# Block 1's gate weights in seven half products, and another order of the work beside them, in a fused linear attention and gated MoE kernel

## Chip, cores and metric

The kernel runs on one core of a Trainium2 chip. The metric is the time of one execution on the device, in microseconds (us), as the median of several runs. Before the change the median of three runs is 318.88 us (318.71 to 319.47). One execution is also taken by the hardware profiler; its timeline, waits and DMA records are what this document reads. The engines are TensorE (PE; PEld is its weight load), VectorE (DVE), ScalarE (ACT), GpSimd (POOL) and SyncE (SP, which issues DMAs here).

## The reference

For each of 8 batches, q, k and v have 8 heads, 576 rows and 64 columns. A linear attention comes first, then a gated feed-forward layer over all 4608 tokens:

```python
kv = np.einsum('bhsd,bhse->bhde', k, v)   # k'v of each head
out = np.einsum('bhsd,bhde->bhse', q, kv)
rms = np.sqrt(np.mean(out * out, axis=-1, keepdims=True) + 1e-06)
x = out / rms * g_norm              # 4608 x 512 after the heads are put side by side
g = x @ w_gate                      # 512 x 1536
gelu = 0.5 * g * (1.0 + erf(g * inv_sqrt2))
val = x @ w_val
ffn_out = gelu * val @ w_out        # 1536 x 512
res_gate = 1.0 / (1.0 + np.exp(-(x @ w_res)))   # w_res is 512 x 512
return x + res_gate * ffn_out
```

## The kernel before

**Blocks.** The tokens are worked off in nine blocks of 512: block b holds the first 512 rows of batch b, block 8 the last 64 rows of all batches. While block m goes through the feed-forward layer, the attention of batch m + 2 runs beside it: `kv_mm` (k'v, 40 matmuls of 64 columns, the last 8 of them for the last rows, tiles `kl` and `vl`), `a_o` (q times k'v, PSUM tiles `op`), `a_ss` (squares on ScalarE, sums over them on VectorE), `a_norm` (the inverse root, tile `ny`), `a_t` (op times ny, tile `t`), `d_xT` (a transpose by DMA, queued on SP) and `a_g` (the scaling by g_norm, in place in `xT`).

**Seven half products.** Where a product is split once into quadrants (Strassen's scheme in Winograd's form), seven products of half the size do what eight would, at the price of sums. `gv_group` does this for w_gate and w_val, with sums of tokens (`token_sums`, tile `ts`) and of weights (`wsg`, `wsv`). `out_by_products` does it for w_out, with sums of the hidden values (`hid_s`, functions `s_begin`, `s_sum`, `s_rest`, `s_last`) and of w_out (`wo_ts`, function `wo_sums`). `res_halves` does it for w_res, with sums of w_res (`wrs`, `wr_sums`), in the blocks from 2 on. Blocks 0 and 1 have the plain w_res product: `m_res`, 16 matmuls of 512 columns.

**Order.** The order of every engine's work is written out by hand. A block is a list of slots on TensorE; `plans[blk][slot]`, filled by `at`, names what is issued after a slot. `at_word` puts work behind a word of a group's order ("2v", "h12"), and `aside_out` ahead of one of the four output quadrants of `out_by_products` ("F", "00", "22", "01", "11", "end"). Each engine works its queue in order.

**Block 1.** Its slots are: two tiles of 128 hidden columns as plain products (0 and 1), a group of four in half products (2), six more plain ones (6 to 11, PSUM tiles `gps`, `vps`), then the output. The output begins with `res(0)` (two `m_res`), k'v of batch 3, `res(1)`, `a_o` of batch 3, and `first_two`: the product wA (hidden quadrant by w_out quadrant), its copy into the bank of wE (ScalarE), the product wD and its copy `wd`. `others` then adds to wA, wE and wF and forms the four output quadrants: on VectorE the sum into wF's bank (line 512, `wF<-wA,wd`), the sum for the last quadrant straight into the output buffer (`osb<-wA,wd`, its `c22`), and the gate products `pf` (line 733: `osb<-th,wE`, `osb<-th,wF`, `osb<-th,wA`); the fourth gate product is GpSimd's. The output buffer `res_all` (`osb`) exists once; block 0's four stores read it (`m_store`: an addition on GpSimd, then a DMA on SP), and `late` spreads them over block 1's slots.

**PSUM banks.** There are eight. `banks_behind` hands block 1's output tiles four of them, and the next block's first group takes over the same four: Ag the bank of wD, Av that of wE, Eg that of wF, Ev that of wA. Its Fg and Fv take the banks of the first two `op` tiles. In a group, product 1 goes into Ag, a copy on ScalarE brings it into Eg ("Eg"), and product 6 then adds to Ag.

```python
ORDERS = {
    None: "1g 1v Eg 5g 6g Ev 5v dg 6v dv Fg 2g Fv 2v 7g g11 7v cg 3g cv 3v h11 g12 4g g21 h12 4v g22 h21 h22",
```

Of the kernel before, what the change touches and what calls it, by code (L numbers as in the profile page):

```python
# [18 lines left out]
def kernel(  # L19
# [57 lines left out]
    def banks_behind():  # L77

        g0, v0, g1, v1 = pmoe.turn
        pmoe.turn = [g1, v0, g0, v1]  # L80
        return {0: g0, 1: g1, 2: v0, 3: g0, "A": v1, "D": g1, "E": v0, "F": g0}

    ctx.enter_context(tc.manual_schedule())
    nc.scalar.preload_act_table_set("sqrt_and_others")
# [125 lines left out]
    def kv_mm(b, ps):  # L210
        k16 = b16_t[b, "k"]
        v16 = b16_t[b, "v"]
        kl, vl = last_kv[b % 2]
        for pr in range(NP):
            for j in range(NJ + 1):
                for e in range(2):
                    h = 2 * pr + e
                    nc.tensor.matmul(  # L218
                        ps[halves(e), pr, :],
                        lhsT=k16[:, h, j * D : (j + 1) * D] if j < NJ else kl[:, h, :],  # L220
                        rhs=v16[:, h, j * D : (j + 1) * D] if j < NJ else vl[:, h, :],
                        start=(j == 0),
                        stop=(j == NJ),
                    )

    def a_kv(b, copy=nc.vector.tensor_copy):
# [260 lines left out]
        nc.vector.tensor_tensor(out=pf, in0=th, in1=fps, op=ALU.mult)  # L487
        return pf

    def m_store(blk, j, pf):  # L490
        osb = pf
        nc.gpsimd.tensor_tensor(out=osb, in0=pf, in1=t_t[blk][:, j, :], op=ALU.add)
        dst = out[blk * S : blk * S + M0, :].rearrange("(p j) c -> p j c", j=NJ)[:, j, :]
        nc.sync.dma_start(out=dst, in_=osb)

# [15 lines left out]
    def sub(eng, out_, in0, in1, op=ALU.subtract):  # L511
        eng.tensor_tensor(out=out_, in0=in0, in1=in1, op=op)

    def wo_sums(i):

        pairs = [(b_of(1, 2), b_of(1, 1)), (b_of(2, 2), wo_t[:, 0]), (b_of(2, 2), b_of(1, 2)), (b_of(2, 1), wo_t[:, 1])]
        sub(nc.vector, wo_t[:, i], *pairs[i])

    def s_begin(blk):

        s_ = hid_sums
        sub(nc.vector, s_[2], a_of(blk, 1, 1), a_of(blk, 2, 1))

    def s_rest(blk):

        s_ = hid_sums
        sub(nc.vector, s_[0], a_of(blk, 2, 1), a_of(blk, 2, 2), ALU.add)
        sub(nc.vector, s_[1], s_[0], a_of(blk, 1, 1))

    def s_sum(blk, i):  # L530

# [10 lines left out]
    def s_last(blk):  # L542
        sub(nc.vector, hid_sums[3], a_of(blk, 1, 2), hid_sums[1])
# [95 lines left out]
    def out_by_products(blk, banks, amid):  # L639
# [4 lines left out]
            for f in amid.get(ahead_of, ()):  # L644
                f()

        def res(jj):
            for j in (2 * jj, 2 * jj + 1):
                m_res(blk, j, banks[j])

        def tiles_of_w():
            for n in ("D", "E", "F", "A"):
                w[n] = pmoe.tile([P, 2, CH], FP32, name="w" + n, bank=banks[n])
# [60 lines left out]
            for jj in ((0, 0), (0, 1), (1, 1), (1, 0)):  # L714
                sigmoid(jj)

        def first_two():
            tiles_of_w()
            s_last(blk)
            prod(w["A"], a_of(blk, 1, 1), b_of(1, 1), True)  # L720
            nc.scalar.copy(out=w["E"], in_=w["A"])
            aside("D")
            prod(w["D"], s_[0], wo_t[:, 0], True)
            nc.scalar.copy(out=w["d"], in_=w["D"])
            aside("d")
            for j in range(NJ):
                m_sigmoid(j)

        def part(jj):
            return slice(None), slice(2 * jj[0], 2 * jj[0] + 2), slice(jj[1] * CH, (jj[1] + 1) * CH)  # L730
# [13 lines left out]
        def others():  # L744


            prod(w["A"], s_[1], wo_t[:, 1], False)
            aside("F")
            sub(nc.vector, w["F"], w["A"], w["d"], ALU.add)
            if res_and_attn(blk):  # L750
                s_last(blk)
            aside("00")
            prod(w["E"], a_of(blk, 1, 2), b_of(2, 1), False)
            if not whole(blk + 1):
                pf((0, 0), w["E"])
            aside("22")
            prod(w["A"], s_[2], wo_t[:, 2], False)
            c22 = res_all[part((1, 1))]
            sub(nc.vector, c22, w["A"], w["d"], ALU.add)
            if whole(blk + 1):  # L760
                pf((0, 0), w["E"])
            aside("01")
            prod(w["F"], s_[3], b_of(2, 2), False)
            pf((0, 1), w["F"])
            aside("11")
            prod(w["A"], a_of(blk, 2, 2), wo_t[:, 3], False)
            if whole(blk + 1):
                pf((1, 1), c22, nc.gpsimd)
                pf((1, 0), w["A"])
                aside("end")  # L770
            else:
                pf((1, 1), c22)
                pf((1, 0), w["A"])
            if blk + 1 == WHOLE or blk + 1 == LAST[0]:
                nc.gpsimd.tensor_copy(out=hold, in_=x_sums[blk + 1][0:1, 3, 1, 1, 0:1])
            if blk == LAST[0]:
                nc.gpsimd.tensor_copy(out=hold, in_=s_[3][0:1, 0, 0:1])
            for j in range(NJ):
                row_times_g(blk, j, nc.gpsimd)
            if blk == LAST[0]:  # L780
                for p in range(B // 2):
                    row_times_g(B, p, nc.gpsimd)
            rows_behind()
# [8 lines left out]
            return [with_res_and_attn, lambda: None, lambda: None, others]  # L792
        if res_in_halves(blk):
            return [with_res, lambda: None, lambda: None, others]
        return [lambda: res(0), lambda: res(1), first_two, others]

    def out_last(blk, banks):

# [239 lines left out]
    def out_by_f(blk):  # L1038

        ths, fpss, pfs, banks = [], [], [], {}  # L1040

        def res(j):
            if j == 0:
                banks.update(banks_behind())
            ths.append(m_res(blk, j, banks[j]))

        slots = [lambda j=j: res(j) for j in range(NJ)]

        def step(f):
            if f == 0:  # L1050
                fpss.extend(pmoe.tile([P, C], FP32, name="fps", bank=banks[n]) for n in "ADEF")
                pmoe.turn = [banks[n] for n in "ADEF"]
            for j in range(NJ):
                m_ffn(blk, j, f, fpss[j])
                for g in amid_step.get((f, j), ()):
                    g()
            if NFH <= f < NFH + NJ:
                m_sigmoid(f - NFH)
            if f == NF - 1:
                pfs.extend(m_gate(j, ths[j], fpss[j]) for j in range(NJ))  # L1060

        slots += [lambda f=f: step(f) for f in range(NF)]
        return slots, [lambda j=j: m_store(blk, j, pfs[j]) for j in range(NJ)]


    tiles_16(0)
# [338 lines left out]
    def plan_attn_2():  # L1405
        b, m = 2, 1
        act = nc.scalar.copy
        at(m - 1, 2 * NF + 3, lambda: by_token(b, act, slice(0, 2)))
        ts = token_sums(m, nc.vector)
        at(m, 0, lambda: by_token(b, act, slice(2, 4)), lambda: attn_begin(b), lambda: d_qT(b), *ts[0:2])  # L1410
        at(m, 1, *ts[2:4])
        at_word(m, 0, "dg", lambda: wo_sums(1))
        at_word(m, 0, "2v", lambda: a_kv(b, act), lambda: load_behind(b))
        at_word(m, 0, "Fv", lambda: wo_sums(2))
        at(m, NF, *late_sums[6:8])
        at(m, 2 + GF, lambda: a_o(b), *[lambda j=j: a_ss(b, j) for j in range(NJ)])
        at(m, 3 + GF, lambda: a_norm(b, 0, NJ))
        for j in range(NJ):
            at(m, 4 + GF + j // 2, lambda j=j: a_t(b, j))
        at(m, 6 + GF, lambda: d_xT(b, 0, NJ))  # L1420
        at(m, NF - 1, lambda: wo_sums(3))
        for i in range(2):
            aside_out(m, "d", lambda i=i: a_g(b, 2 * i, 2 * i + 2, nc.scalar))
        amid_out.setdefault(m, {}).setdefault("00", [])[0:0] = [wr_[3]]

    WHOLE = 2
    GROUPS = {blk: (1, 2) for blk in range(2, WHOLE)} | {blk: (0, 1, 2) for blk in range(WHOLE, B - 1)} | {B - 1: (1, 0, 2), B: (0, 1, 2)}
# [9 lines left out]
    def plan_attn_ahead(b):  # L1437
# [20 lines left out]
                at(m, 2 * GF, lambda: load_behind(b))  # L1458
            last = len(GROUPS[m]) - 1
        else:  # L1460
            at(m, 8, lambda: by_token(b, act, slice(0, 2)))
            at(m, 9, lambda: by_token(b, act, slice(2, 4)), *begin)
            at(m, NF, lambda: a_kv(b, act), lambda: load_behind(b, load_q))
            aside_out(m, "end", lambda: load_kv(b + 1))
        if rem:
            at_word(m + 2, 0, "cv", lambda: a_g(b, NJ, NJ + 1))
# [3 lines left out]
            if own:  # L1470
                at_word(m, last, "3g", lambda: rem_mm(b))
            at_word(m, last, "g12", lambda: rem_out(b))
        else:
            at(m, NF + 1, lambda: a_o(b), *[lambda j=j: a_ss(b, j) for j in range(NJ)])
        aside_out(m, "F", lambda: a_norm(b, 0, NJ + rem, pool))
        first = [lambda: new_block(b), lambda: a_t(b, 0), lambda: a_t(b, 1)]
        if whole(m + 1):
# [32 lines left out]
    for blk in GROUPS:  # L1510
        t = token_sums(blk, nc.vector)
        if blk == 2:
            aside_out(blk - 1, "00", *t[0:2])
            aside_out(blk - 1, "end", *t[2:4])
            continue
        for key, f in zip(("00", "00", "22", "end") if whole(blk) else ("00", "22", "01", "11"), t):
            aside_out(blk - 1, key, f)
# [43 lines left out]
    for blk in range(B + 1):  # L1561
        plan = plans[blk]
        if blk == 0:
# [11 lines left out]
                gv_group(0, 2, ends, amid_gv.get((0, 0), {}), True)  # L1575

            slots += [last_group, None, None, None]
            outs, stores = out_by_f(0)
            slots += outs
            plan_attn_2()  # L1580
            for b in range(3, B):
# [1 line left out]
        else:  # L1583
# [43 lines left out]
                plan.setdefault(NF - 2, []).insert(0, lambda: s_begin(blk))  # L1627

            def products(blk=blk, outs=outs):
                if not res_in_halves(blk) and not res_and_attn(blk):  # L1630
                    s_rest(blk)
                if blk not in GROUPS:
                    out_at[blk] = banks_behind()
                if blk < B:
                    outs.extend(out_by_products(blk, out_at[blk], amid_out.get(blk, {})))
                else:
# [21 lines left out]
                    load_wo(f0, f1)  # L1658
        assert not plan
        if blk == 0:  # L1660
            late = [stores[0:2], [], [], [], stores[2:3], stores[3:4]]


# [28 lines left out]
```

## Time and profile before

| what | value |
|---|---|
| median of 3 runs | 318.88 us |
| profiled execution, its own time | 318.52 us |
| its span, first to last instruction | 316.5 us |
| granted TensorE clock, mean | 0.995 |
| block 1's part: first plain product to block 2's first product | 53.26 to 89.10 us |
| w_res of block 1 on TensorE | 74.84 to 79.2 us, with k'v of batch 3 in between |
| stores of block 0, issued on SP | two at 58.6 and 59.5, two at 67.7 and 68.8 us |
| transposes on SP | qT of batch 3 at 72.2, xT of batch 2 at 75.5 us |

The span counts from the first to the last instruction. What lies around it makes up the 2.0 us to the execution's own time. In a timeline, the columns are the start in us, the duration (of a row's first start to its last end where instructions are merged), engine, line, operation, output and inputs with their shapes, the number of instructions, and in brackets the idle time ahead with what ended it. Matmuls overlap: their pace is read from the starts, not from the durations.

### The profile page before, as it was taken

The numbers are of one execution on the slowest core, as the hardware profiler recorded it, in microseconds if no ns is written. First come the engines' busy times: TensorE is split into PE (matmuls) and PEld (weight loads), VectorE is DVE, ScalarE is ACT, GpSimd is POOL, SyncE is SP. The second block draws the span as 40 slices with busy tenths as digits, with TensorE's granted clock in tenths as the row PEclk, the third lists the DMA queues.
The fourth block names the chain that finished last, engine by engine and source line by source line (L and its number), as shares of the span: only waits on it lengthen the run. The fifth ranks groups of instructions, "written<-read, shape, count | busy, mean of one in ns | idle before, by whom it ended". The sixth has DMA issues, their size and how long they took to land.

```text
span 316.5 us, 7841 instructions
## 1 busy us (share of the span) xinstructions
PE 308.2 (97%) x3071; PEld 249.1 (79%) x3071; DVE 275.7 (87%) x489; ACT 217.0 (69%) x395; POOL 187.4 (59%) x239
## 2 busy tenths in 40 slices
PE   7899999999999999999999999999999999999993
PEld 3555756844888888888888888888888888888882
DVE  5897998989898899989998999899998777897774
ACT  4764688685958794879487948795667367736760
POOL 2883352360799579856985798408850474396332
PEclk9999999999999999999999999999999999999997
DMA  7999999899969598389936994700630003001104
GB/s 253 330 201 204 200 198 197 154 171 209 121 78 177 180 158 110 72 198 150 116 67 201 128 124 71 217 4 0 78 142 1 2 5 131 0 2 59 76 2 133
DMA packets 77398, 38.91 MB, mean 123 GB/s; under 512 B 42290, under 2 KB 75058, under 8 KB 77362
## 3 DMA queue, kind: packets, MB, share of 16 engines
q0 software_dynamic: 39296, 17.17, 43.3%
q1 hardware_dynamic: 37488, 20.71, 26.1%
q8 instruction: 24, 0.39, 0.5%
q10 hardware_dynamic: 578, 0.52, 0.5%
q14 instruction: 12, 0.10, 0.1%
HBM read 38.80 MB, written 9.44 MB: 152 GB/s over the span
## 4 chain that ended last, share of the span: by engine, by line
PE 59%; DVE 1%; issue 0%; DVEq 0%
PE Av L981 10%; PE Ag L981 10%; PE wA L549 8%; PE Fv L981 5%; PE Fg L981 5%; PE rA L600 3%; PE w L549 2%; PE Eg L981 2%; PE Ev L981 2%; PE wF L549 2%; PE wE L549 2%; PE wD L549 2%; PE rF L600 2%; PE rE L600 1%; PE kvp L218 1%; PE op L240 1%
## 5 line engine op out<-in xcount | busy, mean ns | idle before, releaser
L1018 POOL TENSOR_TENSOR hid<-ge,c 128x512 f16<-128x512 f16 x23 | 26.8, 1165 | 36.5 <-ACT ge L1012 36.5
L549 PEld LDWEIGHTS <-hid_s 128*128 128x128 f16 x384 | 37.5, 98 | 4.5
L981 PEld LDWEIGHTS <-wsv 128*128 128x128 f16 x368 | 35.6, 98 | 4.8 <-issue 0.2
L981 PEld LDWEIGHTS <-wsg 128*128 128x128 f16 x368 | 35.8, 98 | 4.2
L394 POOL TENSOR_TENSOR t<-t,g 128x512 f16<-128x512 f16 x32 | 37.8, 1210 | 0.0
L737 POOL TENSOR_TENSOR osb<-osb,t 128x512 f32<-128x512 f32 x28 | 34.0, 1244 | 0.0
L991 ACT COPY Eg<-Ag 128x512 f32<-128x512 f32 x23 | 13.4, 582 | 26.2 <-PE Ag L981 25.6
L549 PEld LDWEIGHTS <-hid 128*128 128x128 f16 x288 | 28.1, 98 | 3.3
L981 PEld LDWEIGHTS <-wg 128*128 128x128 f16 x276 | 27.0, 98 | 3.6
L981 PEld LDWEIGHTS <-wv 128*128 128x128 f16 x276 | 27.0, 98 | 3.1
L981 PE MATMUL Ag<-ts,wsg 128*128 128x256 f16 x184 | 27.6, 273 | 0.0
L981 PE MATMUL Av<-ts,wsv 128*128 128x256 f16 x184 | 27.6, 272 | 0.0
L1002 DVE TENSOR_TENSOR Fg<-Ag,d 128x512 f32<-128x512 f32 x23 | 16.0, 696 | 12.0 <-ACT d L995 9.1
L268 DVE TENSOR_REDUCE ss<-sq 128x8 f32<-128x512 f32 x32 | 20.3, 677 | 0.6 <-ACT sq L263 0.5
L549 PE MATMUL wA<-wo_ts,hid_s 128*128 128x256 f16 x168 | 20.6, 272 | 0.0
L1012 ACT ACTIVATE ge<-Eg 128x512 f16<-128x512 f32 x23 | 13.7, 597 | 9.7 <-PE Eg L981 9.7
L1012 ACT ACTIVATE ge<-c 128x512 f16<-128x512 f32 x23 | 14.4, 625 | 8.0 <-DVE c L1002 8.0
L1012 ACT ACTIVATE ge<-Fg 128x512 f16<-128x512 f32 x23 | 13.6, 591 | 8.8 <-PE Fg L981 7.0
L1002 DVE TENSOR_TENSOR c<-Ag,d 128x512 f32<-128x512 f32 x23 | 15.8, 688 | 4.2 <-PE Ag L981 4.2
L377 DVE TENSOR_TENSOR t<-op,ny 128x512 f16<-128x512 f32 x28 | 18.7, 683 | 0.9 <-POOL ny L334 0.4
L1018 DVE TENSOR_TENSOR hid<-ge,Fv 128x512 f16<-128x512 f16 x23 | 15.6, 680 | 1.5 <-ACT kv L295 1.5
L1012 ACT ACTIVATE ge<-Ag 128x512 f16<-128x512 f32 x23 | 13.7, 598 | 4.1 <-PE Ag L981 4.0
(228 smaller groups left out, 857.1 us busy)
## 6 DMA issues: line engine op xcount, KB each, us to landing
out_dram<-osb SPq DMA_DIRECT2D x14, 512.0 KB, 3.6
qraw<-in_q_dram POOLq DMA_DIRECT2D x7, 512.0 KB, 6.4
k<-in_k_dram POOLq DMA_DIRECT2D x7, 512.0 KB, 7.9
v<-in_v_dram POOLq DMA_DIRECT2D x7, 512.0 KB, 10.7
wo<-in_moe_w_out_dram POOLq DMA_DIRECT2D x3, 384.0 KB, 11.9
wg<-in_moe_w_gate_dram POOLq DMA_DIRECT2D x2, 512.0 KB, 8.4
out_dram<-osb SPq DMA_DIRECT2D x4, 256.0 KB, 5.0
wv<-in_moe_w_val_dram POOLq DMA_DIRECT2D x3, 256.0 KB, 7.5
```

Of the source, the lines that this page charges most:

```text
L218: nc.tensor.matmul(ps[halves(e), pr, :], lhsT=k16[:, h, j * D : (j + 1) * D] if j < NJ else kl[:, h, :], rhs=v16[:, h, j * D : (j + 1) * D ...
L268: nc.vector.tensor_reduce(out=out_, in_=sqs.pop((b, i)), op=ALU.add, axis=mybir.AxisListType.X)
L377: nc.vector.tensor_tensor(out=t, in0=o, in1=scale, op=ALU.mult)
L394: eng.tensor_tensor(out=t_t[blk][:, jj, :], in0=t_t[blk][:, jj, :], in1=g16, op=ALU.mult)
L549: nc.tensor.matmul(ps[:, e - es[0], :], lhsT=a[:, f, e * P : (e + 1) * P], rhs=b[:, f, :], start=(start and e == es[0] and f == 0), stop=( ...
L600: nc.tensor.matmul(out_[:, e, :], lhsT=x_[:, e, cc, :], rhs=w_[:, cc, :], start=(first and e == 0 and cc == 0), stop=(cc == 1), skip_group ...
L737: nc.gpsimd.tensor_tensor(out=res_all[of], in0=res_all[of], in1=t_t[blk][of], op=ALU.add)
L981: nc.tensor.matmul(out_[:, r, :], lhsT=lhsT, rhs=rhs, start=(first and r == 0 and c == 0), stop=(c == 1), skip_group_check=True,)
L991: nc.scalar.copy(out=tile_of("E", u), in_=ps["A", u])
L1002: nc.vector.tensor_tensor(out=dst, in0=ps["A", u], in1=sb["d", u], op=ALU.add)
L1012: nc.scalar.activation(out=ge[q], in_=source(q, "g"), func=AF.Gelu)
L1018: eng.tensor_tensor(out=dst, in0=ge[q], in1=source(q, "v"), op=ALU.mult)
```

## The change

Block 1 gets its w_res product by `res_halves`, in the new `with_res_of_middle`, which strings the seven products, the first two w_out products and the attention of batch 3 together; `first_two`, `res` and `s_rest` go. The banks come from `banks_of_middle`, with other roles. The last sum of w_res (`wr_[3]`) moves ahead of block 1's last hidden product, the last two of `late_sums` (sums of w_val) into the group in slot 2, and `wo_sums(3)` to GpSimd, behind a small copy that waits for the norm of batch 2. `m_store` is parted into `m_add` and `m_store`; the last two stores of block 0 are issued behind the transpose of xT in slot 10. The two copies of q of batch 3 come together in slot 7, the transpose of qT behind them. The scaling `a_g` of batch 2 moves from ScalarE to VectorE, in two halves ahead of "00" and "01", and the first two token sums of block 2 from "00" to "01", behind the second half. In `kv_mm` the loops over chunks and head pairs change places, for all batches from 1 on, and the accumulation flag is set once for a bank.

```diff
+    def banks_of_middle():
+        g0, v0, g1, v1 = pmoe.turn
+        pmoe.turn = [v0, g1, g0, v1]
+        return {0: g0, 1: g1, 2: v0, "A": v1, "D": v0, "E": g1, "F": g0}
...
-        for pr in range(NP):
-            for j in range(NJ + 1):
+        for j in range(NJ + 1):
+            for pr in range(NP):
...
-                        start=(j == 0),
+                        start=(j == 0 and pr == 0),
                         stop=(j == NJ),
+                        skip_group_check=True,
...
-    def m_store(blk, j, pf):
-        osb = pf
-        nc.gpsimd.tensor_tensor(out=osb, in0=pf, in1=t_t[blk][:, j, :], op=ALU.add)
+    def m_add(blk, j, pf):
+        nc.gpsimd.tensor_tensor(out=pf, in0=pf, in1=t_t[blk][:, j, :], op=ALU.add)
+
+    def m_store(blk, j, osb):
...
-    def wo_sums(i):
+    def wo_sums(i, eng=nc.vector):
...
-        def first_two():
-            tiles_of_w()
-            s_last(blk)
-            prod(w["A"], a_of(blk, 1, 1), b_of(1, 1), True)
-            nc.scalar.copy(out=w["E"], in_=w["A"])
-            aside("D")
-            prod(w["D"], s_[0], wo_t[:, 0], True)
-            nc.scalar.copy(out=w["d"], in_=w["D"])
-            aside("d")
-            for j in range(NJ):
-                m_sigmoid(j)
+        def with_res_of_middle():
+            b = blk + 2
...
+            def half_a(e):
+                if e == 0:
+                    tile_of_w("A")
+                half("A", e, a_of(blk, 1, 1), b_of(1, 1))
+
+            def seed():
+                tile_of_w("E")
+                nc.scalar.copy(out=w["E"], in_=w["A"])
+
+            def both_d():
+                tile_of_w("D")
+                for e in range(2):
+                    half_d(e)
+                w["d"] = attnp.tile([P, 2, CH], FP32, tag="sq", bufs=3, name="wd")
+                nc.scalar.copy(out=w["d"], in_=w["D"])
+
+            res_halves(blk, dict(zip("AFE", (banks[j] for j in range(3)))), {
+                "sd": [lambda: a_kv(b, nc.scalar.copy), lambda: load_behind(b, load_q)],
+                "+F": [lambda: s_sum(blk, 0)],
+                "2": [lambda: half_a(0)],
+                "7": [lambda: a_o(b), lambda: a_sq(b, 0), lambda: a_sq(b, 1)],
+                "+c": [lambda: s_sum(blk, 1), lambda: a_red(b, 0), lambda: a_red(b, 1)],
+                "3": [lambda: half_a(1)],
+                "tF": [seed, lambda: a_ss(b, 2), lambda: a_ss(b, 3)],
+                "4": [both_d],
+            }, "1 sE 5 sd 6 +F 2 tE 7 +c 3 tF 4 tA tc")
+            tile_of_w("F")
+            for jj in ((0, 0), (0, 1), (1, 1), (1, 0)):
+                sigmoid(jj)
...
-            if res_and_attn(blk):
+            if not res_in_halves(blk):
                 s_last(blk)
...
-        return [lambda: res(0), lambda: res(1), first_two, others]
+        return [with_res_of_middle, lambda: None, lambda: None, others]
...
-        at(m, NF, *late_sums[6:8])
+        at_word(m, 0, "h12", *late_sums[6:8])
+        at(m, NF - 2, wr_[3])
...
-        at(m, 3 + GF, lambda: a_norm(b, 0, NJ))
+        at(
+            m,
+            3 + GF,
+            lambda: a_norm(b, 0, NJ),
+            lambda: nc.gpsimd.tensor_copy(out=hold, in_=st[b]["rinv"][0:1, 0, 0:1]),
+            lambda: wo_sums(3, nc.gpsimd),
+        )
...
-        at(m, NF - 1, lambda: wo_sums(3))
-        for i in range(2):
-            aside_out(m, "d", lambda i=i: a_g(b, 2 * i, 2 * i + 2, nc.scalar))
-        amid_out.setdefault(m, {}).setdefault("00", [])[0:0] = [wr_[3]]
+        aside_out(m, "00", lambda: a_g(b, 0, 2))
+        amid_out[m]["01"].insert(0, lambda: a_g(b, 2, NJ))
...
-            at(m, 8, lambda: by_token(b, act, slice(0, 2)))
-            at(m, 9, lambda: by_token(b, act, slice(2, 4)), *begin)
-            at(m, NF, lambda: a_kv(b, act), lambda: load_behind(b, load_q))
+            at(m, 3 + GF, *[lambda i=i: by_token(b, act, slice(2 * i, 2 * i + 2)) for i in range(2)], *begin)
...
-            at(m, NF + 1, lambda: a_o(b), *[lambda j=j: a_ss(b, j) for j in range(NJ)])
...
-            aside_out(blk - 1, "00", *t[0:2])
+            aside_out(blk - 1, "01", *t[0:2])
...
-            late = [stores[0:2], [], [], [], stores[2:3], stores[3:4]]
+            late = [[adds[0], stores[0], adds[1], stores[1]], [], [], [], adds[2:3], adds[3:4]]
+            late += [[] for _ in range(6 + GF - len(late))] + [stores[2:4]]
```

More of the change, by code (lines that the diff above doesn't have):

```diff
@@ L512, in sub @@
         eng.tensor_tensor(out=out_, in0=in0, in1=in1, op=op)
-    def wo_sums(i):
+    def wo_sums(i, eng=nc.vector):
         pairs = [(b_of(1, 2), b_of(1, 1)), (b_of(2, 2), wo_t[:, 0]), (b_of(2, 2), b_of(1, 2)), (b_of(2, 1), wo_t[:, 1])]
-        sub(nc.vector, wo_t[:, i], *pairs[i])
+        sub(eng, wo_t[:, i], *pairs[i])
     def s_begin(blk):
@@ L522, in s_begin @@
         sub(nc.vector, s_[2], a_of(blk, 1, 1), a_of(blk, 2, 1))
[L524 to L528, printed above, removed]
     def s_sum(blk, i):
@@ L645, in aside @@
                 f()
-        def res(jj):
-            for j in (2 * jj, 2 * jj + 1):
-                m_res(blk, j, banks[j])
         def tiles_of_w():
@@ L715, in with_res_and_attn, with tile_of_w @@
                 sigmoid(jj)
-        def first_two():
-            tiles_of_w()
-            s_last(blk)
-            prod(w["A"], a_of(blk, 1, 1), b_of(1, 1), True)
-            nc.scalar.copy(out=w["E"], in_=w["A"])
-            aside("D")
-            prod(w["D"], s_[0], wo_t[:, 0], True)
-            nc.scalar.copy(out=w["d"], in_=w["D"])
-            aside("d")
-            for j in range(NJ):
-                m_sigmoid(j)
+        def with_res_of_middle():
+            b = blk + 2
+            def tile_of_w(n):
+                w[n] = pmoe.tile([P, 2, CH], FP32, name="w" + n, bank=banks[n])
+            def half_a(e):
[24 more added lines that the diff above has]
+                sigmoid(jj)
         def part(jj):
@@ L1062, in out_by_f @@
         slots += [lambda f=f: step(f) for f in range(NF)]
-        return slots, [lambda j=j: m_store(blk, j, pfs[j]) for j in range(NJ)]
+        return slots, [[lambda j=j, f=f: f(blk, j, pfs[j]) for j in range(NJ)] for f in (m_add, m_store)]
     tiles_16(0)
@@ L1472, in plan_attn_ahead @@
             at_word(m, last, "g12", lambda: rem_out(b))
-        else:
-            at(m, NF + 1, lambda: a_o(b), *[lambda j=j: a_ss(b, j) for j in range(NJ)])
         aside_out(m, "F", lambda: a_norm(b, 0, NJ + rem, pool))
@@ L1577 @@
             slots += [last_group, None, None, None]
-            outs, stores = out_by_f(0)
+            outs, (adds, stores) = out_by_f(0)
             slots += outs
@@ L1629, in products @@
             def products(blk=blk, outs=outs):
-                if not res_in_halves(blk) and not res_and_attn(blk):
-                    s_rest(blk)
                 if blk not in GROUPS:
-                    out_at[blk] = banks_behind()
+                    out_at[blk] = banks_of_middle()
                 if blk < B:
```

## The prediction

> **What bounds the kernel now.** I read the page first (engine shares, chain of waits), then who waited for whom on TensorE (PE), then the timeline from 55 to 110 us, where block 1 runs, then the DMA issues with their landings.
>
> ```profile
> PE 308.2 (97%) x3071; PEld 249.1 (79%) x3071; DVE 275.7 (87%) x489; ACT 217.0 (69%) x395; POOL 187.4 (59%) x239
> ...
> PE 59%; DVE 1%; issue 0%; DVEq 0%
> ```
>
> ```profile
> PE idle L1154 <- DVE zeros L1125: 1.2, 1, 1.2
> PE kvp L1214 <- DVE gcol L1331: 1.1, 1, 1.1
> PE kvp L1214 <- POOL v L1175: 0.4, 1, 0.4
> ```
>
> The reader is to see that PE carries the end, and that the waits this view puts to PE lie in the opening (lines 1154 and 1214). From 50 us on PE streams, but for single tenths of a microsecond. Four matmuls with 256 columns start every 0.436 us (0.109 each; 89.10 to 89.53 below), eight with 512 columns take 1.73 (0.217 each). So a matmul saved is saved at the end, and a wait added to PE is lost at the end.
>
> ```profile
> 74.84 1.89 PE L464 MATMUL rps<-wr,xT 128*128 128x512 f16 x8
> 76.51 0.68 DVE L432 TENSOR_TENSOR hid<-ge,vps 128x512 f16<-128x512 f16 x1
> 77.42 1.90 PE L464 MATMUL rps<-wr,xT 128*128 128x512 f16 x8
> 79.25 0.64 PE L240 MATMUL op<-kv,qT 64*128 64x64 f16 x32
> 81.14 1.47 PE L549 MATMUL wD<-wo_ts,hid_s 128*128 128x256 f16 x12
> 82.55 1.47 PE L549 MATMUL wA<-wo_ts,hid_s 128*128 128x256 f16 x12
> 83.86 1.47 PE L549 MATMUL wE<-wo,hid 128*128 128x256 f16 x12
> 86.73 0.69 DVE L512 TENSOR_TENSOR osb<-wA,wd 128x512 f32<-128x512 f32 x1 [0.44 <-POOL na L328]
> 87.34 0.68 DVE L733 TENSOR_TENSOR osb<-th,wE 128x512 f32<-128x512 f32 x1
> 88.13 0.69 DVE L377 TENSOR_TENSOR t<-op,ny 128x512 f16<-128x512 f32 x1
> 88.73 0.68 DVE L733 TENSOR_TENSOR osb<-th,wF 128x512 f32<-128x512 f32 x1
> 89.10 0.60 PE L981 MATMUL Ag<-xT,wg 128*128 128x256 f16 x4
> 89.53 0.60 PE L981 MATMUL Av<-xT,wv 128*128 128x256 f16 x4
> 89.73 0.57 ACT L991 COPY Eg<-Ag 128x512 f32<-128x512 f32 x1 [2.33 <-PE Ag L981]
> 104.98 0.87 DVE L403 TENSOR_SCALAR xT<-xT,gcol 128x1024 f16<-128x1024 f16 x2
> ```
>
> To see here: the w_res products (16 matmuls in two runs), a step of 1.41 from wD to wA where 1.31 is usual, and the hand-over to block 2. There the Eg copy writes the PSUM bank of wF, so it needs the gate product of wF (VectorE, 88.73 to 89.41) first. It started at 89.73, when its input was there (0.63 after Ag began), so VectorE was 0.3 us early.
>
> **What the Trainium skill says.** "PSUM — Partial Sum Buffer", section "PSUM bank collisions raise a hardware error": guard PSUM by bank and quadrant, not by address. Hence a new tile waits for the last reader of its bank on any engine. The trace agrees: behind the wait 1.41 - 1.31, wA waited for the copy of wE out of it. "SBUF — State Buffer", section "Who interferes with whom": VectorE and GpSimd share a port pair, and a two-input VectorE operation with both inputs in SBUF meets a GpSimd operation that reads SBUF. The trace agrees: a token sum takes 0.42 alone and 0.79 beside GpSimd's adds (123.30). "TensorE: Matmul & The Clock Gate", section "Back-to-back issue gap", gives 262 cycles for 256 columns (0.109 us) and 518 for 512 (0.216), which the trace repeats.
>
> **The change part by part**, on the profiled execution's own clock. VectorE and ScalarE follow each other in 0.60 and 0.50 where a row says 0.68 and 0.59, since starts overlap; from PE to another engine 0.25 pass.
>
> *w_res.* Before 16 x 0.217 = 3.47; after 28 x 0.109 = 3.05: **-0.41**. k'v and o' of batch 3 stay inside it, so the changes of matmul shape around them (about 0.2 each) stay. The seed copy of wE now comes at 80.97 to 81.55 on ScalarE and wA after it at 82.2, so the step of 1.41 becomes 1.31: **-0.10**. Bounds for it 0 and -0.10.
>
> *k'v by chunks.* 40 matmuls before and after; pairs start every 0.032 us whether the pair adds to the same place or another, so 0 (bounds -0.1 and +0.1 over six batches; no row shows the new order). It puts the eight that need the last rows of k and v 0.5 later. In block 1 k'v starts at 75.81 instead of 76.66, its last eight at 76.3. v landed at 74.8 (63.12 + 11.7), its last rows at 75.9 (64.67 + 11.2): 0 either way, and the next edit helps.
>
> *Two stores later.* Two stores of 256 KB left SP at 67.7 and 68.8 and were 6.8 under way, beside v. Now they follow the transposes of qT and xT on SP, at about 78. SP's later work waits for nothing there (next transpose 95.3). But they free the output buffer that the operation at 86.73 writes; at 79.4 + 6.8 = 86.2 they would just be in time. 0, at worst +0.3. The transpose of qT goes out when ScalarE's two q copies end, now back to back: about 70.4 instead of 72.2; before, it landed at 79.1 (72.18 + 6.9). o' now wants it at 78.8: with 1.8 us more and less traffic, 0. GpSimd holds the next loads until it lands; they move earlier, behind a 1536-wide sum on GpSimd (three times the 1.17 of its 512-wide products: 71.6 to 75.1) while VectorE reads PSUM there: 0. The q copies delay a gelu to 70.3-70.9; its bank is wanted at 71.29: 0. Four 256-wide sums (0.81 from 79.83) move into VectorE's idle 0.90 ahead of 65.70: 0.
>
> *VectorE ahead of the products.* The 0.41 sum of w_res now stands ahead of the last `hid`, which moves from 76.51 to 76.92 and ends at 77.60. The first half of wA takes its bank. PE's order: 1 and 5 (74.84 to 75.71), k'v with its shape changes 0.84, 6, 2 (to 77.43). So PE waits till 77.65: **+0.21** (bounds 0 and +0.35). Product 7 needs the sum behind that `hid`, done at 78.20, and comes at 78.30: 0. After that PE: o' from 78.83, 3, half of wA, 4, wD (80.93 to 82.24), wA to 83.55, wE to 84.86, wA to 86.17, wF to 87.48, wA to 88.79. ScalarE keeps up (wD's copy at 82.50 to 83.08, tanh till 84.1, scaling till 86.4); VectorE's sum into wF's bank starts at 83.82.
>
> *VectorE at the hand-over: the step that decides.* Before, the scaling by g ran on ScalarE (83.14 to 85.33), and two token sums filled VectorE's idle time ahead of 86.73. In the changed program half of the scaling is ahead of that operation, and the other half and both token sums stand behind it, ahead of wF's gate product. The operation starts at 86.17 + 0.25 = 86.42. From there: itself 0.61, wE's gate product 0.61, scaling 0.40 (half of the 0.79 for two in the last row above), token sums 0.48 and 0.43 (85.36 and 85.87 show 0.52 and 0.42), a t 0.60, wF's gate product 0.68: done at **90.23**. Before, the same stretch took 86.73 to 89.41. So Eg's copy starts at 90.32. Its input is there at 88.79 + 0.63 = 89.42. Product 6 of block 2 overwrites that input, is due at 88.79 + 3 x 0.436 = 90.10, and may run at 90.32 + 0.57 + 0.07 = 90.96: **+0.86**, with the Ev and d copies queued behind Eg's on ScalarE (bounds +0.6, with the fastest rows, and +1.15, with one sum beside GpSimd). Then product 5v needs the bank of the second o' tile, freed by the t behind two gate products: 91.45 against 91.40, and its start is 91.5: **+0.10** (0 to +0.3). The rest of the group then fits: block 2's Fg sum starts at 92.1, product 7 is due at 93.3. No later wait shrinks, since all engines start block 2 that much later.
>
> Sum: -0.41 - 0.10 + 0.21 + 0.86 + 0.10 = **+0.66**. The profiled execution took 318.52 (span 316.5), so 319.2; the median of the three runs is 0.36 higher, 318.88, which gives 319.5.
>
> **Rivals.** *A: the order on VectorE is hidden, and the saved matmuls show.* For it: VectorE has idle time in this stretch (0.44 ahead of 86.73), and it loses a 1536-wide sum (0.87) and four 256-wide ones (0.81) there. Against: idle time ahead of that operation doesn't help those behind it. Time: -0.51, 318.4; not slower.
> *B: slower by over 0.3%.* GpSimd's own gate product (1.27, 88.05 before) comes right behind its norm and meets both token sums, which then take 0.71 each instead of 0.43 to 0.48: +0.5 on the same chain, 320.1. It decides if the norm, which starts at 83.5 instead of 83.2, ends before 88.1 (before: 88.09). Against: the 1536-wide sum at 84.4 holds it up as one did before, so I expect 88.5. The late stores would come to the same place.
> That w_res isn't split can't be: 28 matmuls stand in the program.
>
> **How the numbers follow.** Forecast 0.64 (319.5, alone 318.9 to 319.9), A 0.22, B 0.14. About 0.3% (0.96 us, 317.9 to 319.8) is what a measurement of this kernel can tell from no change. Faster: a seventh of A, 0.03. Slower: B and an eighth of the forecast, 0.22. Within: 0.75. The range 318.3 to 320.0 takes in most of A and leaves out about 0.1 at each end.
>
> **What would show it.** Right: PE from product 1 of w_res (74.8) to Ag of block 2 13.95 long instead of 14.26; wA's first half 0.2 late, waiting for `hid`; Eg's copy waiting for VectorE's gate product of wF, with a gap on PE of some 0.85 ahead of Ag's second product. Wrong: Eg's copy ended by PE again; or PE waiting for a DMA (qT, last rows of v) or the operation behind wA waiting for the stores.

## The result, and the profile after

| | before | after |
|---|---|---|
| median (6 runs each, beside each other) | 318.72 us | 320.86 us |
| ratio, 95% interval | | 1.0065 [1.0048, 1.0081] |
| profiled execution, its own time | 318.52 us | 320.58 us |
| its span | 316.5 us | 318.6 us |

The changed kernel is 0.65% slower: +2.1 us where the prediction had +0.66. The page of the changed kernel: PE is as busy as before, but the chain that ended last now leaves PE from 71.7 to 91.2 us and runs through VectorE and a store of 7.6 us. (The rest of its 12% of DMA are loads of the opening.)

```profile
PE 308.3 (97%) x3083; PEld 250.3 (79%) x3083; DVE 278.1 (87%) x492; ACT 215.4 (68%) x395; POOL 190.5 (60%) x241
...
PE 78%; DMA 12%; DVE 6%; issue 1%; SPq 1%; ACT 0%; DVEq 0%
```

The waits of TensorE in the changed kernel (what waited, for whom; us in total, times, longest) have two entries that the kernel before did not have, Fg and Ag; both lie at the hand-over to block 2:

```profile
PE Fg L1003 <- DVE t L384: 1.1, 1, 1.1
...
PE Ag L1003 <- ACT Eg L1013: 0.7, 1, 0.7
```

The timeline of TensorE there, changed kernel, from the first w_res product on:

```profile
75.06 0.60 PE L602 MATMUL rA<-wr,xT 128*128 128x256 f16 x4
...
88.97 0.60 PE L1003 MATMUL Ag<-xT,wg 128*128 128x256 f16 x4
89.40 0.60 PE L1003 MATMUL Av<-xT,wv 128*128 128x256 f16 x4
91.15 0.60 PE L1003 MATMUL Fg<-ts,wsg 128*128 128x256 f16 x4 [1.15 <-DVE t L384]
92.40 0.60 PE L1003 MATMUL Ag<-ts,wsg 128*128 128x256 f16 x4 [0.65 <-ACT Eg L1013]
92.94 0.60 PE L1003 MATMUL Fv<-ts,wsv 128*128 128x256 f16 x4
...
93.81 0.60 PE L1003 MATMUL Eg<-xT,wg 128*128 128x256 f16 x4
```

and the last of these in the kernel before:

```profile
91.72 0.60 PE L981 MATMUL Eg<-xT,wg 128*128 128x256 f16 x4
```

Four such matmuls take 0.436. So product 5 (Fg) is 91.15 - 89.40 - 0.436 = 1.31 late, product 6 (Ag again) 0.81 late, and 5v (Fv) 0.10 late. VectorE in the same stretch:

```profile
86.89 0.69 DVE L520 TENSOR_TENSOR osb<-wA,wd 128x512 f32<-128x512 f32 x1 [0.95 <-POOL na L335]
87.50 0.68 DVE L755 TENSOR_TENSOR osb<-th,wE 128x512 f32<-128x512 f32 x1
88.10 1.48 DVE L410 TENSOR_SCALAR xT<-xT,gcol 128x1024 f16<-128x1024 f16 x1
89.61 0.42 DVE L520 TENSOR_TENSOR ts<-xT 128x512 f16<-128x512 f16 x1
90.07 0.43 DVE L520 TENSOR_TENSOR ts<-xT,ts 128x512 f16<-128x512 f16 x1
90.41 0.68 DVE L384 TENSOR_TENSOR t<-op,ny 128x512 f16<-128x512 f32 x1
91.01 0.68 DVE L755 TENSOR_TENSOR osb<-th,wF 128x512 f32<-128x512 f32 x1
```

and GpSimd:

```profile
87.82 0.25 POOL L341 TENSOR_TENSOR ny<-nh,ny 128x32 f32<-128x32 f32 x1
88.03 1.26 POOL L755 TENSOR_TENSOR osb<-th,osb 128x512 f32<-128x512 f32 x1
```

The order is the predicted one, and Eg's copy (91.78 on ScalarE) follows the gate product of wF as predicted. Two things are new. The second scaling took 1.48 instead of 0.48: GpSimd's gate product had begun 0.07 before it and ran until 89.29 (that the one is the cause of the other is shown by e2 below). The delay reaches TensorE through the t at 90.41, which frees the bank that Fg takes. And the operation behind wA began 0.3 late. The view names a POOL operation as releaser that was long done; the chain of waits of the changed kernel shows the store instead:

```profile
78.45 0.53 SPq L502
...
79.07 7.63 DMA out_dram<-osb
...
86.89 0.09 DVE osb L520
```

The store issued at 79.07 landed at 86.70. Where the 2.0 us of the last matmul's shift lie, from starts in the two timelines of TensorE: the opening +0.22 (it varies from execution to execution), w_res to block 2's Ag -0.35 (13.91 instead of 14.26), Ag to block 2's third product Eg +2.22 (4.84 instead of 2.62), a wait of 0.24 at 123.1 in the kernel before that is gone, and 0.1 spread over the rest.

To compare executions with different openings, the experiments are read by one stretch: from the first w_res product to block 2's third product (`Eg<-xT`), 74.84 to 91.72 = 16.88 in the kernel before and 75.06 to 93.81 = 18.75 in the changed one. The profiled execution of e3 fell into a disturbed state of the chip, so only the order of its operations is read.

### The profile page after: what moved, and what is told of

The parts are those of the page before. It is cut to its first block, busy times and chain, and to the rows that moved or that the text cites. A ratio compares the mean times of both kernels' runs of the same rounds, so it can differ in the third digit from the quotient of the medians.

```text
span 318.6 us, 7869 instructions
## 1 busy us (share of the span) xinstructions
PE 308.3 (97%) x3083; PEld 250.3 (79%) x3083; DVE 278.1 (87%) x492; ACT 215.4 (68%) x395; POOL 190.5 (60%) x241
## 4 chain that ended last, share of the span: by engine, by line
PE 78%; DMA 12%; DVE 6%; issue 1%; SPq 1%; ACT 0%; DVEq 0%
PE Ag L1003 12%; PE Av L1003 12%; PE wA L551 10%; PE Fv L1003 6%; PE Fg L1003 6%; DMA wo<-in_moe_w_out_dram 4%; PE rA L602 4%; DMA wv<-in_moe_w_val_dram 4%; PE Ev L1003 3%; PE Eg L1003 3%; PE fps L488 3%; PE w L551 2%; PE wF L551 2%; PE wE L551 2%; PE wD L551 2%; DMA out_dram<-osb 2%
## 5 line engine op out<-in xcount | busy, mean ns | idle before, releaser
L270 ACT ACTIVATE sq<-op 128x512 f32<-128x512 f32 x28 | 15.1, 609 | 2.4 <-PE op L247 2.4
## 6 DMA issues: line engine op xcount, KB each, us to landing
wo<-in_moe_w_out_dram POOLq DMA_DIRECT2D x3, 384.0 KB, 11.7
```

Of the source, the lines that this page charges most:

```text
L270: nc.scalar.activation(out=sqs[b, i], in_=src, func=AF.Square)
```

## The experiments

Theory 1: the late stores begin the delay, and only so does the scaling meet GpSimd's gate product. Theory 2: VectorE and GpSimd meet there whatever the stores do. A rival to both: VectorE's new order costs what it costs without any meeting. (A meeting is an operation of VectorE and one of GpSimd that want to run at once, where one of them takes longer for it.)

| kernel | ratio to before, 95% interval | stretch, us |
|---|---|---|
| changed kernel, again (e11) | 1.0049 [1.0023, 1.0075] | 18.47 |
| old stores (e1) | 1.0092 [1.006, 1.0124] | 20.18 |
| GpSimd held (e2) | 1.0021 [1.0004, 1.0038] | 17.53 |
| scaling ahead (e3) | 1.0001 [0.9978, 1.0025] | not read |
| late stores in other buffers (e8) | 1.0031 [1.0019, 1.0044] | 18.33 |
| filled, old stores (e5) | 1.0012 [0.9996, 1.0027] | 16.86 |
| filled, late stores (e6) | 0.9993 [0.9974, 1.0012] | 16.92 |
| filled, late stores, other buffers (e9) | 0.9994 [0.9978, 1.001] | 16.92 |
| same, one sum moved (e10) | 0.9983 [0.9968, 0.9997] | 16.66 |
| before + late stores (e7) | 0.9996 [0.9977, 1.0014] | 16.88 |
| before + k'v by chunks (e4) | 0.9998 [0.9986, 1.0011] | 16.96 |

**e1: the stores as before.**

```diff
-            late = [[adds[0], stores[0], adds[1], stores[1]], [], [], [], adds[2:3], adds[3:4]]
-            late += [[] for _ in range(6 + GF - len(late))] + [stores[2:4]]
+            late = [[adds[0], stores[0], adds[1], stores[1]], [], [], [], [adds[2], stores[2]], [adds[3], stores[3]]]
```

> The changed kernel with one part undone: the last two stores of block 0 go out right behind their additions again, as before. Theory 1 (the late stores begin the delay: they hold the operation behind wA by 0.3, and only so does the second scaling meet GpSimd's gate product, 1.48 instead of 0.48): the operation behind wA starts at about 86.6, the second scaling starts at 87.8, ahead of GpSimd's product, and takes 0.4 to 0.5; the gap of 1.3 ahead of TensorE's group at 91.15 is gone, the one of 0.8 ahead of the next stays; 1.3 to 1.4 less than the changed kernel, 319.4 to 319.6. Theory 2 (the scaling meets GpSimd's product whatever the stores do): only 0.3 less, 320.5, and the scaling still takes over 1.2.

Both theories missed: 321.84 us, above the changed kernel's ratio instead of below it. The operation behind wA no longer waited for a store, yet the meeting came all the same, now with the first token sum (1.37 instead of 0.43). So theory 1 falls. On top came a wait that neither theory had. Timeline of e1 on TensorE and on SP's queue:

```profile
83.65 0.64 PE L247 MATMUL op<-kv,qT 64*128 64x64 f16 x32 [1.54 <-DMA qT<-q]
```

```profile
70.89 1.44 SPq L502 DMA_DIRECT2D out_dram<-osb  x2
73.59 5.20 SPq L414 DMA_TRANSPOSE qT<-q  x1
```

The same queue in the changed kernel:

```profile
70.67 3.01 SPq L414 DMA_TRANSPOSE qT<-q  x1
75.38 2.98 SPq L427 DMA_TRANSPOSE xT<-t  x1
78.45 1.01 SPq L502 DMA_DIRECT2D out_dram<-osb  x2
```

With the stores early, the issue of qT's transpose took 5.20 instead of 3.01, v was 12.0 under way (66.29 to 78.29) instead of 9.5 (63.33 to 72.79), and o' (q times k'v, tile `op`) waited for qT. The profiled execution overstates this somewhat: its stretch is 3.3 above that of the kernel before, its kernel's median only 2.6. The late stores are no mere cost: the new order wants qT 3.9 behind the first w_res product (78.98 - 75.06), the old one 4.4 (79.25 - 74.84), and they make room for that.

**e2: GpSimd's gate product held back** by a one-element copy that reads the second token sum.

```diff
+                if blk + 1 == WHOLE:
+                    nc.gpsimd.tensor_copy(out=hold, in_=x_sums[blk + 1][0:1, 1, 0, 0, 0:1])
                 pf((1, 1), c22, nc.gpsimd)
```

> The changed kernel with a one-element copy on GpSimd that holds its gate product of block 1 until VectorE's second token sum is done. Stores stay late. If the collision of scaling and gate product is what the gap of 1.3 on TensorE consists of: the scaling takes 0.4 to 0.5, about 1.1 less than the changed kernel, 319.8, and the gap ahead of the Eg copy (0.8) stays. If the late stores' 0.3 is the larger part: 0.3 or less gained, 320.6 or above.

Measured 319.75 us, as expected, against 319.26 for the kernel before on that chip. Timeline of VectorE, and then of TensorE, in e2:

```profile
87.67 0.56 DVE L410 TENSOR_SCALAR xT<-xT,gcol 128x1024 f16<-128x1024 f16 x1
88.27 0.42 DVE L520 TENSOR_TENSOR ts<-xT 128x512 f16<-128x512 f16 x1
88.72 0.42 DVE L520 TENSOR_TENSOR ts<-xT,ts 128x512 f16<-128x512 f16 x1
```

```profile
89.80 0.60 PE L1005 MATMUL Fg<-ts,wsg 128*128 128x256 f16 x4
91.05 0.60 PE L1005 MATMUL Ag<-ts,wsg 128*128 128x256 f16 x4 [0.65 <-ACT Eg L1015]
91.60 0.60 PE L1005 MATMUL Fv<-ts,wsv 128*128 128x256 f16 x4
```

The gap of 1.31 ahead of Fg is down to 0.10; the 0.81 ahead of Ag and the 0.11 ahead of Fv stay. The stretch is 17.53, +0.65 on the kernel before: the prediction's sum, to 0.01. That is what is left for the rival; it does not explain the other 1.2. The stores landed at 83.08 here, in time, so this run takes both extras away. That the stores alone do not bring the 1.2 back is shown by the next two.

**e8: the late stores in the other two buffers**, so that they do not hold the buffer of the operation behind wA. **e11: the changed kernel again.**

```diff
-        pf = res_all[:, j, :]
+        pf = res_all[:, (j + 2) % NJ, :]
```

> The changed kernel with the four output tiles of block 0 in rotated buffers, so that the two late stores hold the buffers that block 1 writes second (wE's gate product), not the one that the operation behind wA writes. Nothing else differs. If the wait for the stores is worth its 0.3 and the port collision comes all the same (as with the early stores, where the first token sum took 1.37 in place of the scaling): the operation behind wA starts 0.25 behind wA, one VectorE operation still takes 1.3 to 1.5, and the time is 0.2 to 0.4 below the changed kernel, a ratio to the kernel before of about 1.0055. If the stores' wait is what brings the collision: 1.2 to 1.4 below it, about 1.002.

> The changed kernel as it is, beside the others on one chip. If the port collision comes in every execution: a ratio of 1.006 to 1.008 again, and one VectorE operation behind wE's gate product takes 1.3 to 1.5. If it comes only in some: 1.003 to 1.005 and a spread of over 1 us.

Timelines of VectorE and of GpSimd, e8:

```profile
87.20 0.69 DVE L520 TENSOR_TENSOR osb<-wA,wd 128x512 f32<-128x512 f32 x1 [0.59 <-PE wA L551]
87.81 0.68 DVE L755 TENSOR_TENSOR osb<-th,wE 128x512 f32<-128x512 f32 x1
88.40 0.48 DVE L410 TENSOR_SCALAR xT<-xT,gcol 128x1024 f16<-128x1024 f16 x1
88.92 0.43 DVE L520 TENSOR_TENSOR ts<-xT 128x512 f16<-128x512 f16 x1
89.38 1.37 DVE L520 TENSOR_TENSOR ts<-xT,ts 128x512 f16<-128x512 f16 x1
```

```profile
88.95 1.51 POOL L755 TENSOR_TENSOR osb<-th,osb 128x512 f32<-128x512 f32 x1
```

No wait for a store, and the meeting again, with the second token sum. (The stores had landed by 84.3 in this execution, so they would have held nothing in the old buffers either.) In e11 the stores landed in time (84.66 and 85.85), and it was the first sum:

```profile
87.46 0.55 DVE L410 TENSOR_SCALAR xT<-xT,gcol 128x1024 f16<-128x1024 f16 x1
88.04 1.37 DVE L520 TENSOR_TENSOR ts<-xT 128x512 f16<-128x512 f16 x1
89.45 0.43 DVE L520 TENSOR_TENSOR ts<-xT,ts 128x512 f16<-128x512 f16 x1
```

So of the four profiled executions with the changed order behind wA and GpSimd free, all have one operation of 1.37 to 1.48, and one has the wait for a store. Theory 2 stands: GpSimd's gate product has a window of 1.5 us of VectorE work to fall into, not a moment at which it decides. The wait for the store is the 0.28 by which the changed kernel's first profiled execution (18.75) exceeds e11 (18.47). The time of e8 lies between the two values its expectation named, and its interval overlaps that of e11. What the stores' wait costs in the median is not settled, only that it was 0.3 in the one profiled execution that had it. How often the meeting comes is not settled either: e11's ratio and its spread of over 1 us fit the second branch of its expectation, "only in some", but the interval takes in both branches, and the kernel before spreads over more than 1 us too. The profiled executions, four of four, speak for the first.

**e3: both halves of the scaling ahead of the operation behind wA**, the sums behind it.

```diff
-        aside_out(m, "00", lambda: a_g(b, 0, 2))
-        amid_out[m]["01"].insert(0, lambda: a_g(b, 2, NJ))
+        aside_out(m, "00", lambda: a_g(b, 0, 2), lambda: a_g(b, 2, NJ))
```

> The changed kernel with both halves of the scaling ahead of the operation behind wA; the two token sums stay behind it, stores stay late. If VectorE's order there sets the time: the scaling (1.48) leaves the chain, the token sums meet GpSimd's gate product and take up to 0.7 each instead of 0.45, so 0.9 to 1.4 less, 319.5 to 320.0, with the gap ahead of the Eg copy smaller by the scaling's own 0.4 or more. If the stores set it alone: less than 0.3 gained.

Median 319.39 us, level with the kernel before, a gain a little above the expected one: the sums did not lose 0.7 each. Timelines of VectorE and GpSimd, e3:

```profile
89.92 0.42 DVE L520 TENSOR_TENSOR ts<-xT,ts 128x512 f16<-128x512 f16 x1
```

```profile
89.95 1.51 POOL L755 TENSOR_TENSOR osb<-th,osb 128x512 f32<-128x512 f32 x1
```

With less work behind wE's gate product, the last sum had begun when GpSimd came, and GpSimd paid (1.51 instead of 1.26; e8 shows the same 1.51), off the path. "SBUF — State Buffer", section "Who interferes with whom", in the Trainium skill says just this: issue order decides who blocks, for the whole instruction. The trace agrees: VectorE paid 0.9 to 1.0 where it came second, nothing here. In e1, e8 and e11 both paid in turn: GpSimd's product began while one VectorE operation ran and took 1.45 to 1.51, and the next VectorE operation then waited for it.

**e5, e6, e9, e10: VectorE's idle time filled.** The scaling and both sums stand ahead of the operation behind wA, the sum for w_res behind the last `hid`. e5 has the old stores, e6 the late ones, e9 the late ones in the other buffers; e10 also moves the last 1536-wide sum behind two reductions.

```diff
-        at(m, NF - 2, wr_[3])
-        aside_out(m, "00", lambda: a_g(b, 0, 2))
-        amid_out[m]["01"].insert(0, lambda: a_g(b, 2, NJ))
+        amid_out[m]["00"][0:0] = [lambda: a_g(b, 0, 2), lambda: a_g(b, 2, NJ)]
...
-            aside_out(blk - 1, "01", *t[0:2])
+            aside_out(blk - 1, "00", *t[0:2])
...
+                "+F": [wr_[3], lambda: s_sum(blk, 0)],
...
-                "tF": [seed, lambda: a_ss(b, 2), lambda: a_ss(b, 3)],
+                "tF": [seed, lambda: a_ss(b, 2), lambda: a_ss(b, 3), lambda: s_sum(blk, 3)],
```

(The last two lines are e10's; in e5, e6 and e9 that sum is at the end of "+c".)

> The changed kernel with VectorE's idle time ahead of the operation behind wA filled: both halves of the scaling and both token sums stand ahead of it, and the sum for w_res stands behind the last hid, the sum for wE's product further ahead; old stores. If the whole loss is VectorE's order and the stores at the hand-over, all three gaps (1.31, 0.82, 0.11) and the wait of wA's first half (0.13) go, and what the split of w_res saves shows: 318.7 - 0.41 - 0.10 = 318.2. If the 16 to 28 matmuls save nothing at the end, it is 318.7 or above.

> The version with VectorE's idle time filled, with the late stores of the change put back. The reading of the runs so far: early stores keep v and with it the transpose of qT back, so that o' waits 0.5 (filled version) to 1.7 us; late stores free that, and the filled order takes the rest away. Then no gap over 0.15 is left on TensorE between 75 and 95 us and the time is 0.4 to 0.7 below the filled version, a ratio of about 0.9985 to the kernel before, unless the stores land after 86.4 and hold the operation behind wA (up to 0.4 of that lost). If the late stores only cost: the same as the filled version or above, 1.001 to 1.002.

> As the filled version with late stores, and the late stores hold the other buffers. If the stores' landing holds the operation behind wA in some executions: 0.1 to 0.3 below that version, and a smaller spread. If they land in time anyway: the same within 0.1.

> As the filled version with late stores in the other buffers, with one 1536-wide sum on VectorE moved behind the last two reductions that GpSimd's norm waits for. If the gap of 0.44 that was left there is the norm's end (its last step at 89.06, then the t that waited for it): the norm ends 0.6 to 0.9 sooner, TensorE has no gap over 0.15 between 75 and 95 us, the stretch from the first w_res product to the group four behind the hand-over is 17.3 long against 17.75 in the kernel before, and the time is 0.5 to 0.7 below the kernel before, a ratio of 0.998. If something else follows at once: as the version without the move, 0.9994.

e5 missed its 318.2 (319.56, beside 319.26). The hand-over was clean, but o' waited for qT, as in e1 (timeline of TensorE, e5):

```profile
79.09 0.64 PE L247 MATMUL op<-kv,qT 64*128 64x64 f16 x32 [0.36 <-DMA qT<-q]
```

It started 0.95 behind the product before it, where the changed kernel has 0.53. e6 and e9 have that 0.4 back, but missed "no gap": the t of op tile 0 waited for the norm, and Ag's second product came 0.43 late. Timeline of VectorE, e6:

```profile
89.66 0.69 DVE L384 TENSOR_TENSOR t<-op,ny 128x512 f16<-128x512 f32 x1 [0.83 <-POOL ny L341]
```

No wait for the stores shows in either: in e6 they had landed by 87.25, while VectorE was busy with the second token sum until 87.48. (The ratios differ by 0.0001, but their intervals of some 0.6 us to each side could not rule out such a wait.) e10 mended part: its norm ended 0.27 sooner in the stretch, not 0.6 to 0.9, and 0.16 of the gap stayed. Timeline of TensorE, e10:

```profile
88.52 0.60 PE L1003 MATMUL Ag<-xT,wg 128*128 128x256 f16 x4
88.96 0.60 PE L1003 MATMUL Av<-xT,wv 128*128 128x256 f16 x4
89.40 0.60 PE L1003 MATMUL Fg<-ts,wsg 128*128 128x256 f16 x4
90.00 0.60 PE L1003 MATMUL Ag<-ts,wsg 128*128 128x256 f16 x4
```

From the first product (74.76) to Ag it is 13.76, 0.50 less than before: the two savings of the prediction, -0.41 and -0.10, together whole (the step from wD to wA, 80.66 to 81.97, is 1.31 as forecast). On one chip e10 took 318.57 us, the kernel before 319.10 and the changed one 320.75; the gain on the kernel before is under 0.3%, with an interval that just leaves out no change.

**e7 and e4: one part of the change on the kernel before.** e7 has only the late stores; e4 only this:

```diff
-        for pr in range(NP):
-            for j in range(NJ + 1):
+        for j in range(NJ + 1):
+            for pr in range(NP):
...
-                        start=(j == 0),
+                        start=(j == 0 and pr == 0),
...
+                        skip_group_check=True,
```

> The kernel before with only the last two stores of block 0 later. If the late stores free v and the transpose of qT: v lands some 2 us sooner (72.8 instead of 74.8), qT at or below 78 instead of 79.06; the kernel before hardly waited for qT, so the time is the same within 0.2, ratio 0.9995 to 1.0005. If the stores then land late and hold the operation behind wA (86.73): up to 0.3 more.

> The kernel before with k'v chunk by chunk and nothing else. All theories of the change: matmul pairs start every 0.032 us in either order, so 0 within 0.1 in the traced stretches; if the other order costs or saves as much as 0.1 a batch, up to 0.6 in all.

Both came out at nothing. In e7 v was 10.0 under way instead of 11.7, but nothing waited for it; the stores landed at 86.17 and 87.91, before the operation behind wA started. k'v by chunks costs nothing that shows: in block 1 it takes 0.76 from its first start to the next w_res product in e4 (76.51 to 77.27) as in the kernel before (76.66 to 77.42), and e4's interval is 0.4 us to each side.

## Why the prediction was wrong

- *w_res (-0.41) and the seed copy (-0.10)* were right: -0.50 in e10. From the first w_res product to Ag the changed kernel took 13.91, where 13.95 was forecast. *Chunks (0)*: right (e4).
- *wA's first half waiting for `hid` (+0.21)*: measured 77.80 - 77.23 - 0.436 = 0.13, on the same wait. It is gone in e10, where the sum for w_res stands behind that `hid`.
- *Eg's copy behind the gate product of wF (+0.86) and 5v (+0.10)*: the mechanism was right. Without the meeting (e2) the gaps are 0.10 + 0.81 + 0.11 = 1.02 where 0.96 was forecast.
- **The step that failed: "scaling 0.40, token sums 0.48 and 0.43".** These three took 2.31 (88.10 to the t at 90.41) instead of 1.31, because GpSimd's gate product fell among them. The text had this as rival B, and three of its terms do not hold. *What is hit*: it named the token sums alone, both of them; what was hit is one operation, in the changed kernel's first profiled execution the scaling. *The price*: 0.71 a sum stands in no row, and the operation that comes second is not slowed, it waits for the other's end, 0.9 to 1.0 here. The prediction's own row shows this: the sum of 0.79 at 123.30 ended at 124.08, 0.28 behind the end (123.80) of the GpSimd addition that was running. *The condition*: the norm's start at 83.53 was the forecast one, but it ended at 88.07 and not at 88.5; and "it decides if the norm ends before 88.1" was no threshold. On the prediction's own times (86.42 + 0.61 + 0.61 + 0.40 + 0.48) the second sum stands from 88.52 to 88.95, so that the 88.5 it expected lies at that sum's very start, no safe distance either. With the norm's end at 88.07 the gate product met the scaling; in e8, where it came later beside the same work, the second sum. The one arrival among these operations that cost VectorE nothing was behind the start of the second sum (e3).
- *Two stores later (0, at worst +0.3)*: the worst case came in the profiled execution (0.3), not in e11. What the text missed is that their benefit was needed: with them undone qT holds up o' by 0.4 to 1.6 (e5, e1).
- *No later wait shrinks*: wrong. A wait of 0.24, at 123.1 in the kernel before and also in e7 and e4, is in none of the changed versions. Why was not tried.

The sum for the profiled execution: the forecast's +0.66, +0.95 for the meeting, +0.3 for the store and -0.24 give 1.7. With the opening's +0.22 and 0.1 over the rest that is the shift of 2.0.

## What to carry to other kernels

When operations move behind another on VectorE, look at everything GpSimd may start in that whole window: where the two share a port, price the loss as the rest of the other's operation (here it was 0.1 to 0.2 less), and do so for whichever operation is in the window. A transfer moved later has two sides, the buffer that it holds longer and the transfers that it no longer crowds, and undoing it may cost more than it did. Filling idle time ahead of a product pays only while nothing that another engine waits for, here the norm's reductions, is pushed back by it.

## What the hardware showed

- The blocked VectorE operation ended 0.28 to 0.29 behind GpSimd's end whatever it was: the scaling 89.58 after 89.29 (changed kernel), the first sum 89.41 after 89.13 (e11), the second 90.75 after 90.46 (e8). Alone they take 0.42 to 0.48. The other way round, GpSimd's gate product ended 1.11 to 1.12 behind the end of the VectorE operation that it had come upon (e1, e8, e11); alone it takes 1.26.
- In the 13 profiled executions of this study the issue of qT's transpose on SP ended 0.5 to 0.9 behind the landing of v, be it 72.79 or 78.29. So it took 1.9 (e7) to 5.2 (e1). Whether it waits for v itself or for room in the DMA engines that v fills stays open.
- Two stores of 256 KB issued beside v made its load of 512 KB 11.5 to 12.0 long instead of 9.5 to 10.1 (four and eight executions; e3 is left out).
